# Two pairs of chunks at the start of a state-space and PReLU kernel: C in blocks turned by VectorE, and running products picked by a selection matmul

## The chip, the cores and the metric

The kernel runs on one core of a Trainium2 chip. The metric is the device time of one execution in microseconds (us); lower is better. Engines are named as in the profile: PE is TensorE (matmuls), PEld its weight loads, DVE is VectorE, ACT is ScalarE, POOL is GpSimd, and SP is SyncE, which issues most DMAs; ACT issues four small ones at the start.

## What is computed

Two blocks follow each other. The first is a chunked state-space scan over 4 batches, 8 heads, 768 tokens, head width 32 and 16 states; the second is a feed-forward layer with a PReLU of one slope per hidden unit:

```python
# first block, per batch and head, chunk by chunk
cum = cumsum(log(clip(a)))                 # within the chunk
L   = exp(cum_i - cum_j) * (i >= j)        # products of a between two tokens
y_i = sum_j (C_i . B_j) L_ij x_j  +  (C_i . state) * exp(cum_i)
state = exp(cum_last) * state + sum_j B_j x_j * exp(cum_last - cum_j)
# second block, on y as 3072 tokens x 256
h = y @ w_in                               # 256 x 2048
g = max(h, 0) + alpha * min(h, 0)
out = g @ w_out                            # 2048 x 256
```

All data is fp32.

## The kernel before, in words

The kernel cuts the tokens into chunks of 128 and works on them in twelve pairs. Two pairs make a group of 512 tokens for the feed-forward layer. Almost the whole span is the feed-forward layer on PE, with the pairs of later groups worked off between its matmuls. All engines run in the order in which the program is written (a manual schedule); an engine that waits holds everything behind it.

The first two pairs have a path of their own, `first_two` (line 821). They are cut into four quarters of 64 tokens each. For pair 0 it goes like this:

- `load_pair(0)` issues the loads. B and C come token by token, 64 bytes per head and token (line 192), x likewise in 128 bytes (line 197), a once as rows of 128 tokens (`rows`, 96 of them, line 126) and once repeated over the 16 states of each head (`ap`, line 133).
- `spread` (line 865) copies each head's a to all 64 tokens of a quarter by matmuls, and `scan` (line 871) on DVE makes the products of a between two tokens (`dec`).
- `rows_short` (line 488) scans the 96 rows twice on DVE: `pr` holds products from a token to its quarter's end, `rpf` the running products from the quarter's start. `pr` is turned by PE and copied by ACT (`prt`, line 511), and POOL multiplies B by it (`bn`, line 533).
- The running products are also needed with one row per head and state. For pair 0 they come from a scan of `ap` on DVE (`pf0`, line 1000). For pair 1 `rpf` is written to memory (`short`, line 500) and read back repeated over the states (`load_second`, line 231).
- `turned` (line 837) turns B and C on PE (line 843) into two PSUM banks, and ACT copies them to `bc` (line 847), C first; `spread_c` (line 854) makes two masked copies of C on ACT (`cz`).
- `gram_of` (line 881) multiplies B and C on PE, `times` (line 887) multiplies the result by `dec` on DVE, `added` (line 895) makes the new states' sums on PE, `states` (line 910) adds them up on DVE with the running products, `mask` (line 916) spreads them on POOL, `decayed_c` (line 961) multiplies C by the running products on POOL, and `x_products` (line 929) and `state_products` (line 941) make y on PE, which ACT copies to `xT` (lines 949 and 950).

Pair 1 follows in the same way, interleaved with the conversion of the first weights. A piece of w_in arrives as `raw`; ACT makes `wt` and `wg` (lines 273 and 283), DVE `wr` (lines 296 and 308), POOL or DVE clamps `wt` (line 278), and POOL adds the halves into `w_in` (line 330). `hidden_two` (line 1110) starts the feed-forward matmuls of the first 256 tokens; it stands before and around pair 1's work, and its second call runs pair 1's `gram_of` and y matmuls between its own. `keep_warm` (line 338) are matmuls on constants whose result nobody reads.

In PSUM, `spare()` gives one of two banks of the tag `hp`; a bank's first 256 columns and the rest are used for different things, for instance B's turned copy in front and `keep_warm` or the states' sums (`dps_in`) behind.

Of the kernel before, what the change touches and what calls it, by code (L numbers as in the profile page):

```python
# [22 lines left out]
def kernel(  # L23
# [32 lines left out]
    P = 128  # L56
# [82 lines left out]
    def load_tokens(dst, src, t0):  # L139


        d = dst.rearrange("p j (h w) -> p j h w", h=H)
        for k in range(2):
            for j in range(2):
                t = t0 + k * Q + j * HQ
                nc.sync.dma_start(out=d[HQ * k : HQ * (k + 1), j],
                                  in_=src[:, t : t + HQ, :].rearrange("h p w -> p h w"))
# [22 lines left out]
    def load_pair(gp, decays=True, parted=False):  # L170


        b, c = divmod(2 * gp, CPB)
        turned = gp > GC
        nat = ldx.tile([P, 3, 2, H * N], F32, name="nat")
        xt = ldx.tile([P, 2, HD], F32, name="xt")

        ap = ldx.tile([P, 2 * Q], F32, name="ap")
        if gp == 0:
            load_a(ap, b, c)  # L180
        elif gp > NB:
            load_products(gp, ap)
        if gp == 0:
            load_rows(0, nc.scalar)
        abc = []
        if gp >= HALF:
            load_tokens(nat[:, 0], B[b], c * Q)
        def load_bc(k):
            ts = slice((c + k) * Q, (c + k + 1) * Q)
            for i, src in enumerate((B,) if turned else (B, C)):  # L190
                eng = nc.scalar if gp == 0 and i else nc.sync
                eng.dma_start(out=nat[:, i, k].rearrange("p (h n) -> p h n", h=H),  # L192
                              in_=src[b, :, ts, :].rearrange("h p n -> p h n"))

        def load_x(k):
            ts = slice((c + k) * Q, (c + k + 1) * Q)
            nc.sync.dma_start(out=xt[:, k].rearrange("p (h d) -> p h d", h=H),  # L197
                              in_=x[b, :, ts, :].rearrange("h p d -> p h d"))

        for k in range((1 if parted else 2) if gp < HALF else 0):  # L200
            load_bc(k)
            if gp >= NB:
                load_x(k)
        for k in range(2 if gp < NB else 0):
            load_x(k)
        if gp == 0:
            nc.scalar.dma_start(out=al_n, in_=moe_alpha.rearrange("(k p) -> k p", p=P))
            loads["a", 1] = prep.tile([P, 2 * Q], F32, name="a1")
            load_a(loads["a", 1], b, c + 2)
        for i, src in enumerate((B, C) if turned else ()):  # L210


            for e in range(2):
                first = src[b, e : e + 1, c * Q : (c + 2) * Q, :]
                nc.sync.dma_start(out=nat[:, 1 + e, i],
                                  in_=bass.AP(tensor=first.tensor, offset=first.offset,
                                              ap=[[2 * S * N, P // 32], [8 * N, 32], [1, 8 * N]]))
        for k in range(2 if gp >= NB else 0):
            abc.append(lda.tile([P, H * Q], F32, name="abc"))
        loads["p", gp] = nat, abc, xt, ap  # L220
        if gp >= HALF:
            load_tokens(xt, x[b], c * Q)
        if decays:
            for part in load_spread(gp, b, c):
                pass
        return lambda: load_bc(1), lambda: load_x(1)

    def load_second():

        rows = scratch["short", 0].rearrange("(b h c) t -> b h (c t)", b=2, h=H)  # L230
        nc.sync.dma_start(out=loads["p", 1][3], in_=rows[0, :, 2 * Q : 4 * Q].unsqueeze(1)
                          .to_broadcast([H, N, 2 * Q]))

    al_n = const.tile([NF, P], F32, name="al_n")
    load_pair(0)
# [99 lines left out]
    def keep_warm(to, n, cols=2 * Q):  # L335

        for i in range(n):
            nc.tensor.matmul(to[:, :cols], warm.to_broadcast([P, P]), warm.to_broadcast([P, cols]),
                             start=True, stop=True, skip_group_check=True)
# [11 lines left out]
    lent = [gp.tile([P, 4, Q], F32, name="gt", tag="gt") for i in range(4)]  # L351
    starts_r = lent[3][:, 1]
    nc.gpsimd.memset(starts_r, 0.0)
    starts_a = lent[0][:, :2].rearrange("p k t -> p (k t)")
    nc.gpsimd.memset(starts_a, 0.0)
    bmask = const.tile([P, HD], F32, name="bmask")
    nc.gpsimd.memset(bmask, 1.0)
    bm3 = bmask.rearrange("p (h d) -> p h d", h=H)
# [7 lines left out]
    nc.vector.reduce_sum(out=par, in_=bm2[:, :, :, 0], axis=mybir.AxisListType.X)  # L366
    hmask = bmask[:, :P]
    nc.gpsimd.tensor_tensor(out=hmask, in0=hmask, in1=bmask[:, P:], op=ALU.add)
    zeros = const.tile([P, Q], F32, name="zeros")
    nc.gpsimd.memset(zeros, 0.0)  # L370
    ends = const.tile([P, Q], F32, name="ends")
# [14 lines left out]
    def slopes(alp):  # L386
        over = const.tile([P, NF], F32, name="over")
        nc.gpsimd.tensor_scalar(out=over, in0=alp, scalar1=1.0, scalar2=None, op0=ALU.is_gt)
        nc.gpsimd.tensor_scalar(out=s_mul, in0=over, scalar1=-2.0, scalar2=1.0, op0=ALU.mult,
                                op1=ALU.add)  # L390
        nc.gpsimd.tensor_tensor(out=s_alpha, in0=alp, in1=s_mul, op=ALU.mult)
# [44 lines left out]
    def clamp(eng, out, in_):  # L436
        eng.tensor_scalar(out=out, in0=in_, scalar1=1e-6, scalar2=1.0, op0=ALU.max, op1=ALU.min)
# [50 lines left out]
    def rows_short(r):  # L488


        nc.vector.memset(r[:, ::HQ], 0.0)
        pr = lent[3][:RW, 2]
        nc.vector.tensor_tensor_scan(out=pr[:, ::-1], data0=r[:, 1:][:, ::-1],
                                     data1=ends_q[:RW, ::-1], initial=0.0, op0=ALU.mult,
                                     op1=ALU.add)
        rpf = lent[3][:RW, 3]
        nc.vector.tensor_tensor_scan(out=rpf, data0=r[:, :Q], data1=starts_r[:RW], initial=0.0,
                                     op0=ALU.mult, op1=ALU.add)
        scratch["short", 0] = dr.tile([RW, Q], F32, name="short0")
        nc.sync.dma_start(out=scratch["short", 0], in_=rpf)  # L500
        return pr

    def rows_turn(i, pr):

# [316 lines left out]
    def first_two():  # L821
# [4 lines left out]
        nat0, _, xt0, ap0 = loads["p", 0]  # L826
        dec = [work.tile([P, 2, H, Q], F32, name="dec").rearrange("p k h t -> p (k h t)")
               [:, : 8 * Q].rearrange("p (r c) -> p r c", r=4) for i in range(2)]
        pf0 = lent[0][:, 2:].rearrange("p k t -> p (k t)")
        new = [lent[2][:, 2 * i : 2 * i + 2].rearrange("p k (c m) -> p (k c) m", c=2)  # L830
               for i in range(2)]
        sm = xsp.tile([P, 4, HT], F32, name="xs")
# [1 line left out]
              for i in range(2)]  # L834
        halves = [slice(HQ * j, HQ * (j + 1)) for j in range(2)]

        def turned(nat, banks, warmed=False):


            bc = work.tile([P, 4, Q], F32, name="bc")  # L840
            for k in range(2):
                for i, tp in enumerate(banks):
                    nc.tensor.transpose(tp[:, k * P : (k + 1) * P], nat[:, i, k], ident)
                if warmed and k == 0:
                    keep_warm(banks[0][:, 2 * Q :], 1)
            for i in (1, 0):
                nc.scalar.copy(out=bc[:, 2 * i : 2 * i + 2].rearrange("p k t -> p (k t)"),
                               in_=banks[i][:, : 2 * Q])
            return bc

        def spread_c(bc):
            cz = czp.tile([P, 2, 2, Q], F32, name="cz")
            for e in range(2):
                nc.scalar.mul(cz[:, e].rearrange("p k t -> p (k t)"),
                              bc[:, 2:].rearrange("p k t -> p (k t)"), par[:, e : e + 1])
            return cz
# [116 lines left out]
        clamp(nc.vector, rq[:, :Q], rows)  # L973
        z0 = first_a(ap0, nc.vector, lent[1][:, :2])
        clamp(nc.gpsimd, starts_r[:RW, ::HQ], rows[:, ::HQ])
        clamp(nc.gpsimd, starts_a[:, ::HQ], ap0[:, ::HQ])
        rows_clamp(0)
        sp = [bank(r) for r in range(4)]
        spread(z0, sp)
        prq = rows_short(rq)  # L980
        rows_out(0)
        load_pair(1)
        load_second()
        nat1, _, xt1, pf1 = loads["p", 1]
        for r in range(4):
            scan(0, r, sp[r])
        rows_turn("short", prq)
        tp, hp = spare(), spare()
        bc0 = turned(nat0, (tp, hp), True)
        cz0 = spread_c(bc0)  # L990
        al_p = ss()
        nc.tensor.transpose(al_p[:, :NF], al_n, ident[:NF, :NF])
        keep_warm(al_p[:, Q:], 1, 3 * Q)
        nc.scalar.copy(out=alpha, in_=al_p[:, :NF])
        bn0 = pair_loads(0)
        slopes(alpha)
        gram_of(bc0, cz0, sp)
        dps = dps_in([hp, tp])
        added(dps, bn0, xt0)
        nc.vector.tensor_tensor_scan(out=pf0, data0=z0.rearrange("p k t -> p (k t)"),  # L1000
                                     data1=starts_a, initial=0.0, op0=ALU.mult, op1=ALU.add)
        cd0 = decayed_c(bc0, pf0)
        for r in (0, 1):
            times(0, r, sp[r])
        states(0, dps, pf0)
# [27 lines left out]
        convert_b(*pieces[1])  # L1033
        for r in (2, 3):
            scan(1, r, sp[r])
        bn1 = pair_loads(1)
        convert_next(first=False)
        own = [ss(), ss()]
        second = spare()
        bc1 = turned(nat1, (sp[0], second))  # L1040
        cz1 = spread_c(bc1)
        dps = dps_in(own)
        mask(0, slice(3, 4))
        slope_signs()
# [535 lines left out]
```

## Time and profile before

| What | Value |
|---|---|
| three runs | 356.01, 356.4 and 356.7 us; median 356.4 |
| profiled execution, from the first to the last instruction | 355.9 us |
| granted TensorE clock | 1.000 |
| PE busy | 349.3 us (98%) |
| DVE, POOL, ACT busy | 235.8, 204.4 and 171.8 us |
| DMA packets | 105581, of them 79896 under 512 bytes |

The page gives the profiled execution by its span. The runs' median lies 0.5 us above that span, and what lies around the span is taken as that 0.5 us. The chain of waits names for each moment the work that the end depended on; "SPq" in it is the issuing of DMAs. The busy time of PE contains matmuls that run behind one another in a pipeline, so that a busy share near 100% does not by itself say that no time is lost.

### The profile page before, as it was taken

How to read it: one execution, taken by the hardware profiler on the slowest of the kernel's cores; microseconds unless marked ns; L12 is line 12 of the kernel's file. 1: busy time of each engine (PE TensorE's matmuls, PEld its weight loads, DVE VectorE, ACT ScalarE, POOL GpSimd, SP SyncE). 2: the span in 40 equal slices, each digit the busy share in tenths (PEclk: the TensorE clock that was granted, in tenths of full speed). 3: DMA queues.
4: the chain of work that ended last, by engine and by line, in shares of the span. 5: the costliest groups of instructions: out<-in, count | busy, mean ns of one | idle time of the engine just before them, and what ended most of it. 6: DMA issues, size and time to landing. Idle time of an engine off the chain costs nothing.

```text
span 355.9 us, 7778 instructions
## 1 busy us (share of the span) xinstructions
PE 349.3 (98%) x2985; PEld 284.4 (80%) x2985; DVE 235.8 (66%) x482; ACT 171.8 (48%) x391; POOL 204.4 (57%) x228
## 2 busy tenths in 40 slices
PE   8899999999999999999999999999999999999996
PEld 4576665578788888888888888888888888888885
DVE  6876986998748756847747856757856633643363
ACT  3477576535355346345345445345445344443431
POOL 6776568589939855725646626637526535434520
PEclk9999999999999999999999999999999999999999
DMA  7899989607345403503423423422001001001102
GB/s 138 182 202 270 329 174 279 148 17 159 106 83 128 102 3 75 104 2 77 78 57 74 86 51 71 85 55 65 11 2 31 0 2 29 2 1 31 31 0 59
DMA packets 105581, 30.24 MB, mean 85 GB/s; under 512 B 79896, under 2 KB 101448, under 8 KB 105544
## 3 DMA queue, kind: packets, MB, share of 16 engines
q1 hardware_dynamic: 103048, 29.43, 36.3%
q10 hardware_dynamic: 2496, 0.32, 0.6%
q8 instruction: 23, 0.38, 0.5%
q14 instruction: 14, 0.11, 0.1%
HBM read 26.32 MB, written 3.42 MB: 84 GB/s over the span
## 4 chain that ended last, share of the span: by engine, by line
PE 89%; SPq 4%; DMA 3%; DVE 2%; ACT 1%; POOL 1%; issue 0%; DVEq 0%; ACTq 0%
PE bank L1216 33%; PE hp L1241 29%; PE bank L1142 6%; PE ss L1241 6%; PE hp L1095 3%; DMA raw<-in_moe_w_in_dram 2%; SPq L192 2%; PE ss L787 1%; PE ss L731 1%; PE hp L1110 1%; PE bank L1209 1%; PE ss L805 1%; PE ss L779 1%; DMA xt<-in_x_dram 1%; SPq L197 1%; PE ss L742 1%
## 5 line engine op out<-in xcount | busy, mean ns | idle before, releaser
L1298 POOL TENSOR_TENSOR gt<-gt 128x512 f32<-128x512 f32 x58 | 74.2, 1279 | 21.1 <-DVE gt L1226 16.3
L1216 PE MATMUL bank<-gt,w_out 128*128 128x256 f32 x320 | 83.5, 381 | 0.0
L1216 PEld LDWEIGHTS bank<-gt,w_out 128*128 128x128 f32 x320 | 60.1, 190 | 9.2 <-issue 1.0
L1288 POOL TENSOR_TENSOR gt<-gt 128x512 f32<-128x512 f32 x20 | 25.4, 1269 | 62.5 <-DVE gt L1226 49.7
L1226 DVE SCALAR_TENSOR_TENSOR gt<-hp,s_mul,gt 128x256 f32<-128x256 f32 x96 | 42.0, 479 | 29.1 <-ACT gt L1224 26.8
L1224 ACT ACTIVATE gt<-hp,s_alpha 128x256 f32<-128x256 f32 x96 | 40.3, 471 | 34.5 <-PE hp L1241 31.4
L1216 PE MATMUL bank<-gt,ws 128*128 128x256 f32 x224 | 55.9, 379 | 0.0
L1216 PEld LDWEIGHTS bank<-gt,ws 128*128 128x128 f32 x224 | 42.3, 190 | 5.6
L1241 PE MATMUL hp<-xs,w_in 128*128 128x256 f32 x160 | 41.9, 384 | 0.0
L1241 PE MATMUL hp<-xs,ws 128*128 128x256 f32 x160 | 41.1, 380 | 0.0
L1267 DVE TENSOR_TENSOR hp<-hp,u 128x512 f32<-128x512 f32 x20 | 14.0, 700 | 35.2 <-ACT u L1265 35.2
L1241 PEld LDWEIGHTS hp<-xs,ws 128*128 128x128 f32 x160 | 30.3, 190 | 4.3 <-POOL xs L1183 0.2
L1241 PEld LDWEIGHTS hp<-xs,w_in 128*128 128x128 f32 x160 | 29.7, 190 | 4.5
L1142 PE MATMUL bank<-w_out,gt 128*128 128x256 f32 x128 | 31.1, 385 | 0.4 <-POOL w_out L330 0.4
L1142 PEld LDWEIGHTS bank<-w_out,gt 128*128 128x128 f32 x128 | 23.6, 190 | 7.2 <-issue 2.9
L1241 PE MATMUL ss<-xT,w_in 128*128 128x256 f32 x96 | 24.6, 379 | 0.0
L645 POOL TENSOR_TENSOR sm<-state,bmask 128x256 f32<-128x256 f32 (+1 forms) x10 | 6.2, 620 | 29.0 <-DVE state L642 29.0
L1095 PE MATMUL hp<-xT,w_in 128*128 128x512 f32 x48 | 22.8, 596 | 0.0
L561 DVE TENSOR_TENSOR_SCAN dec<-abc,bank 128x192 f32<-128x192 f32 x48 | 22.7, 522 | 0.0
L1256 ACT COPY m<-hp 128x512 f32<-128x512 f32 x8 | 4.7, 586 | 35.7 <-PE hp L1241 35.7
L1265 ACT COPY u<-hp 128x512 f32<-128x512 f32 x20 | 11.7, 585 | 19.4 <-PE hp L1241 19.4
L1226 DVE SCALAR_TENSOR_TENSOR gt<-c,s_mul,gt 128x256 f32<-128x256 f32 x40 | 20.6, 555 | 0.0
(232 smaller groups left out, 608.2 us busy)
## 6 DMA issues: line engine op xcount, KB each, us to landing
abc<-z SPq DMA_DIRECT2D x24, 192.0 KB
raw<-in_moe_w_in_dram SPq DMA_DIRECT2D x8, 512.0 KB
raw<-in_moe_w_out_dram SPq DMA_DIRECT2D x8, 512.0 KB
abc<-z SPq DMA_DIRECT2D x8, 512.0 KB
out_dram<-o_sb SPq DMA_DIRECT2D x32, 64.0 KB
nat<-in_B_dram SPq DMA_DIRECT2D x26, 64.0 KB
xt<-in_x_dram SPq DMA_DIRECT2D x12, 128.0 KB
xt<-in_x_dram SPq DMA_DIRECT2D x24, 64.0 KB
```

What stands on the lines that cost most here:

```text
L192: eng.dma_start(out=nat[:, i, k].rearrange("p (h n) -> p h n", h=H), in_=src[b, :, ts, :].rearrange("h p n -> p h n"))
L561: nc.vector.tensor_tensor_scan(out=dv[:, o : o + SQ], data0=abc[k][:, s : s + SQ], data1=ident_p[0][:, :SQ], initial=0.0, op0=ALU.mult, op ...
L1095: nc.tensor.matmul(hp, w_in[:, k, f * P : (f + 1) * P], xts[g][:, k], start=(k == 0), stop=(k == KC - 1))
L1142: nc.tensor.matmul(pos[0][t // 2][:, t % 2], gt[:, t * Q : (t + 1) * Q], w_out[:, f], start=(f == 0 and t % 2 == 0), stop=(f == NF - 1), s ...
L1216: nc.tensor.matmul(ms[g][i][:, h], w, blocks[g, z][n][:, p], start=(q == 0 and h == 0), stop=(q == NQ - 1), skip_group_check=True)
L1224: nc.scalar.mul(o[:, p], h[:, p], s_alpha[:, fs[p]])
L1226: nc.vector.scalar_tensor_tensor(out=o[:, p], in0=h[:, p], scalar=s_mul[:, fs[p]], in1=o[:, p], op0=ALU.mult, op1=ALU.max)
L1241: nc.tensor.matmul(to[:, p], w(2 * z + p), b, start=start and p == 0, stop=True, skip_group_check=True)
L1265: nc.scalar.copy(out=u2, in_=A)
L1267: nc.vector.tensor_tensor(out=Y, in0=Y, in1=u2, op=ALU.add)
L1288: nc.gpsimd.tensor_tensor(out=tc_, in0=g22, in1=g12, op=ALU.subtract)
L1298: eng.tensor_tensor(out=o, in0=x0, in1=x1, op=ALU.subtract)
```

## The change

For pairs 0 and 1, C is now loaded in blocks of eight tokens (512 bytes; two DMAs per pair in place of two), the form in which the later pairs are loaded, and turned by one DVE transpose per pair, `turn_c`; B is still turned by PE (`turn_b`). The running products of both pairs no longer come from a scan of `ap` (pair 0) or through memory (pair 1): a matrix `pick` of zeros and ones, made on POOL, selects and repeats the rows of `rpf` in four 128-column matmuls, two for each pair (`products_of`), and ACT copies the two results. One `keep_warm` of 384 columns goes, POOL's clamp into `starts_a` goes, and `added` stands before `gram_of` in pair 0.

```diff
-            for i, src in enumerate((B,) if turned else (B, C)):
-                eng = nc.scalar if gp == 0 and i else nc.sync
+        if gp < NB:
+            load_blocks(lambda e: nat[:, 1, e], C, nc.scalar if gp == 0 else nc.sync)
+            for i, src in enumerate((B,) if turned or gp < NB else (B, C)):
...
-    def load_second():
-        rows = scratch["short", 0].rearrange("(b h c) t -> b h (c t)", b=2, h=H)
-        nc.sync.dma_start(out=loads["p", 1][3], in_=rows[0, :, 2 * Q : 4 * Q].unsqueeze(1)
-                          .to_broadcast([H, N, 2 * Q]))
...
-    starts_a = lent[0][:, :2].rearrange("p k t -> p (k t)")
-    nc.gpsimd.memset(starts_a, 0.0)
+    pick = lent[0][:RW]
+    nc.gpsimd.memset(pick, 0.0)
...
     nc.gpsimd.tensor_tensor(out=hmask, in0=hmask, in1=bmask[:, P:], op=ALU.add)
+    pick4 = pick.rearrange("p k (h n) -> p k h n", h=H)
+    nc.gpsimd.affine_select(out=pick4, in_=pick4, pattern=[[-1, 4], [-CPB, H], [0, N]],
+                            compare_op=ALU.not_equal, fill=1.0, base=0, channel_multiplier=1)
...
-        scratch["short", 0] = dr.tile([RW, Q], F32, name="short0")
-        nc.sync.dma_start(out=scratch["short", 0], in_=rpf)
-        return pr
+        return pr, rpf
...
+        def turn_c(nat):
+            bc = work.tile([P, 4, Q], F32, name="bc")
+            nc.vector.transpose(
+                bc[:, 2:].rearrange("p k t -> p (k t)").rearrange("p (c b) -> p b c", b=8),
+                nat[:, 1].rearrange("p e (b n) -> p b e n", n=N))
+            return bc
+        def turn_b(bc, nat, tp):
+            for k in range(2):
+                nc.tensor.transpose(tp[:, k * P : (k + 1) * P], nat[:, 0, k], ident)
+            nc.scalar.copy(out=bc[:, :2].rearrange("p k t -> p (k t)"), in_=tp[:, : 2 * Q])
+        def products_of(c, tp):
+            pf = prep.tile([P, 2 * Q], F32, name=f"pf{c}")
+            for k in range(2):
+                nc.tensor.matmul(tp[:, k * P : (k + 1) * P], pick[:, c + k], rpq,
+                                 start=k == 0, stop=True, skip_group_check=True)
+            nc.scalar.copy(out=pf, in_=tp[:, : 2 * Q])
+            return pf
...
-        clamp(nc.gpsimd, starts_a[:, ::HQ], ap0[:, ::HQ])
...
         load_pair(1)
-        load_second()
+        bc0 = turn_c(nat0)
+        cz0 = spread_c(bc0)
         for r in range(4):
             scan(0, r, sp[r])
         rows_turn("short", prq)
         tp, hp = spare(), spare()
-        bc0 = turned(nat0, (tp, hp), True)
-        cz0 = spread_c(bc0)
+        turn_b(bc0, nat0, tp)
+        keep_warm(tp[:, 2 * Q :], 1)
+        pf0 = products_of(0, hp)
+        pf1 = products_of(2, ss())
         al_p = ss()
         nc.tensor.transpose(al_p[:, :NF], al_n, ident[:NF, :NF])
-        keep_warm(al_p[:, Q:], 1, 3 * Q)
         nc.scalar.copy(out=alpha, in_=al_p[:, :NF])
         bn0 = pair_loads(0)
+        cd0 = decayed_c(bc0, pf0)
         slopes(alpha)
-        gram_of(bc0, cz0, sp)
         dps = dps_in([hp, tp])
         added(dps, bn0, xt0)
-        nc.vector.tensor_tensor_scan(out=pf0, data0=z0.rearrange("p k t -> p (k t)"),
-                                     data1=starts_a, initial=0.0, op0=ALU.mult, op1=ALU.add)
-        cd0 = decayed_c(bc0, pf0)
+        gram_of(bc0, cz0, sp)
...
         for r in (2, 3):
             scan(1, r, sp[r])
+        bc1 = turn_c(nat1)
+        cz1 = spread_c(bc1)
         bn1 = pair_loads(1)
         convert_next(first=False)
         own = [ss(), ss()]
         second = spare()
-        bc1 = turned(nat1, (sp[0], second))
-        cz1 = spread_c(bc1)
+        turn_b(bc1, nat1, second)
```

More of the change, by code (lines that the diff above doesn't have):

```diff
@@ L187, in load_pair, with load_blocks @@
             load_tokens(nat[:, 0], B[b], c * Q)
+        def load_blocks(to, src, eng=nc.sync):
+            for e in range(2):
+                first = src[b, e : e + 1, c * Q : (c + 2) * Q, :]
+                eng.dma_start(out=to(e),
+                              in_=bass.AP(tensor=first.tensor, offset=first.offset,
+                                          ap=[[2 * S * N, P // 32], [8 * N, 32], [1, 8 * N]]))
+        if gp < NB:
+            load_blocks(lambda e: nat[:, 1, e], C, nc.scalar if gp == 0 else nc.sync)
         def load_bc(k):
             ts = slice((c + k) * Q, (c + k + 1) * Q)
-            for i, src in enumerate((B,) if turned else (B, C)):
-                eng = nc.scalar if gp == 0 and i else nc.sync
-                eng.dma_start(out=nat[:, i, k].rearrange("p (h n) -> p h n", h=H),
-                              in_=src[b, :, ts, :].rearrange("h p n -> p h n"))
+            for i, src in enumerate((B,) if turned or gp < NB else (B, C)):
+                nc.sync.dma_start(out=nat[:, i, k].rearrange("p (h n) -> p h n", h=H),
+                                  in_=src[b, :, ts, :].rearrange("h p n -> p h n"))
         def load_x(k):
@@ L210, in load_pair @@
         for i, src in enumerate((B, C) if turned else ()):
[L213 to L217, printed above, removed]
+            load_blocks(lambda e: nat[:, 1 + e, i], src)
         for k in range(2 if gp >= NB else 0):
@@ L828, in first_two @@
                [:, : 8 * Q].rearrange("p (r c) -> p r c", r=4) for i in range(2)]
-        pf0 = lent[0][:, 2:].rearrange("p k t -> p (k t)")
         new = [lent[2][:, 2 * i : 2 * i + 2].rearrange("p k (c m) -> p (k c) m", c=2)
@@ L835, in first_two @@
         halves = [slice(HQ * j, HQ * (j + 1)) for j in range(2)]
-        def turned(nat, banks, warmed=False):
+        def turn_c(nat):
             bc = work.tile([P, 4, Q], F32, name="bc")
-            for k in range(2):
[L842 to L849, printed above, removed]
+            nc.vector.transpose(
[3 more added lines that the diff above has]
+        def turn_b(bc, nat, tp):
+            for k in range(2):
+                nc.tensor.transpose(tp[:, k * P : (k + 1) * P], nat[:, 0, k], ident)
[7 more added lines that the diff above has]
+            return pf
         def spread_c(bc):
@@ L979, in first_two @@
         spread(z0, sp)
-        prq = rows_short(rq)
+        prq, rpq = rows_short(rq)
         rows_out(0)
         load_pair(1)
-        load_second()
-        nat1, _, xt1, pf1 = loads["p", 1]
+        nat1, _, xt1, _ = loads["p", 1]
+        bc0 = turn_c(nat0)
+        cz0 = spread_c(bc0)
         for r in range(4):
```

## The prediction

> **What bounds the kernel now.** First the busy time of the engines on the page (busy us, share, instructions), which names PE.
>
> ```profile
> PE 349.3 (98%) x2985; PEld 284.4 (80%) x2985; DVE 235.8 (66%) x482; ACT 171.8 (48%) x391; POOL 204.4 (57%) x228
> ```
>
> Then two stretches; the columns are length, busy time of PE, PEld, DVE, ACT and POOL, granted clock, DMA share and GB/s.
>
> ```profile
> 23.20:46.00 22.80, 22.35 (x102) 14.46 (x101) 17.70 (x35) 16.11 (x35) 14.72 (x16) 1.00 0.96 276
> 46.00:355.90 309.90, 306.50 (x2500) 257.32 (x2500) 200.01 (x399) 145.94 (x333) 173.42 (x173) 1.00 0.30 65
> ```
>
> From 46 us on PE is busy for 306.50 of 309.90 us, and from 23.2 to 46 for 22.35 of 22.80. The change touches nothing there, so the end moves by what PE is late or early on leaving the first two pairs, at 23.28 us, less what later stalls give back. The chain in order of time (start, length, what) shows how PE gets there, and that later stall.
>
> ```profile
> 14.22 3.28 DMA xt<-in_x_dram
> 17.54 0.35 PE ss L895 x16
> 17.89 0.63 PE hp L338 x2
> 18.52 0.86 PE hp L1110 x4
> 19.38 0.65 PE bank L881 x32
> 29.84 7.45 DMA raw<-in_moe_w_in_dram
> 44.52 1.28 POOL w_out L330
> 45.84 1.99 PE bank L1142 x8
> ```
>
> Pair 1's x lands at 17.50 and starts `added`, the second keep_warm, L1110 and gram in turn. At 45.8 a chain that began with a weight's load ends; PE loses about 0.45 us there (45.4 to 45.84), and a later PE loses that much less. Last, the timeline by engine (start, busy time, engine, line, operation, and in brackets the idle time before it with its releaser).
>
> ```profile
> 4.02 0.24 POOL L437 TENSOR_SCALAR gt<-rows 96x2 f32<-96x2 f32 x1
> 4.55 0.39 DVE L497 TENSOR_TENSOR_SCAN gt<-rq,gt 96x128 f32<-96x128 f32 x1
> 5.55 2.43 DVE L871 TENSOR_TENSOR_SCAN dec<-bank,ident_q 128x256 f32<-128x256 f32 x4 [0.61 <-PE bank L865]
> 5.79 0.24 ACT L511 COPY prt<-ss 128x96 f32<-128x96 f32 x1 [0.81 <-PE ss L506]
> 7.30 0.92 ACT L854 ACTIVATE cz<-bc,par 128x256 f32<-128x256 f32 x2
> 8.97 0.76 DVE L887 TENSOR_TENSOR dec<-bank,dec 128x256 f32<-128x256 f32 x2 [0.40 <-PE bank L881]
> 12.24 0.43 DVE L278 TENSOR_SCALAR wt<-wt 128x512 f32<-128x512 f32 x1 [0.28 <-ACT wt L273]
> 13.28 1.69 POOL L330 TENSOR_TENSOR w_in<-wr,wg 128x256 uint32<-128x256 uint32 x2 [2.13 <-ACT xT L949]
> 16.31 1.26 DVE L871 TENSOR_TENSOR_SCAN dec<-bank,ident_q 128x256 f32<-128x256 f32 x2
> 17.06 0.37 ACT L847 COPY bc<-hp 128x256 f32<-128x256 f32 x1 [2.51 <-PE hp L843]
> 18.30 0.98 DVE L910 SCALAR_TENSOR_TENSOR gt<-gt,ap,ss 128x64 f32<-128x64 f32 x3 [0.72 <-DMA ap<-short]
> ```
>
> The reader should see that in pair 1 DVE is busy with scans until 17.57, while ACT copies C at 17.06, straight after PE turned it. C's new way lies behind those scans.
>
> **The price of the new steps.** The turn on DVE handles 128x256 elements, read and written with strides. Its nearest rows are L574, the same operation and pattern at 128x512, with 1108 to 1120 ns, and L1392, contiguous, with 702 for 128x512 and 434 for 128x256. I take half of L574's with a little for the start, 0.60 us; bounds 0.43 and 1.11. A pick costs two fp32 matmuls of 128 columns: a 256-column fp32 pass took 0.21 us here (eight L1110 in 1.73), so 0.43 for the two and their filling, then ACT's copy of 0.37 (L847), or 0.25 to 0.3 where it follows other work on ACT (17.06 to 17.33). POOL's select over 96x512 has as rows 0.29 us for 128 columns (the identity's, at 1.07) and 0.45 for 256 (L361): 0.16 per 128 columns, 0.77 at 512. The memset for `pick` covers 512 columns where `starts_a` had 256; memset rows of 0.20 (128) and 0.31 (256) give 0.22 more.
>
> **Pair 0.** POOL comes first. Before its `starts_r` clamp (L437, ending 4.27) now stand the memset's 0.22 and the select's 0.77: it ends at about 5.2. The second scan of the rows waits for it and ends at 5.65 in place of 4.94. The new turn stands behind that on DVE, 6.25, provided that both C loads have landed (C was there for PE at 5.59). ACT runs in order, so `cz` (0.92) from 6.25 to 7.2 now holds the copy of `prt` (7.4, before 6.03) and B's copy (0.25, 7.65). Behind B's copy waits keep_warm, which writes the other half of B's bank; it cannot start before that copy in the changed program. Queued behind it on PE are both picks, alpha's turn, `added` and gram.
>
> keep_warm's 0.60 gives 8.3, the picks 8.8, `pf0`'s copy 9.2. `added`, which shares the pick's bank, runs from 9.45 to 10.0 and gram from 9.95; before, gram ran from 8.27. `times` follows 0.7 after gram's start: 10.6 in place of 8.97, +1.65. The next link takes some back: the first weight's clamp on DVE (L278) waited 0.28 us for ACT's `wt` at 12.24 and comes at 13.6, +1.35. The weights' adds on POOL (L330) go from 13.28 to 14.65, and the scans of pair 1, behind the same DVE work, end at 18.95 in place of 17.57. PE's first L1110 moves along.
>
> **Pair 1.** `turn_c` is put behind the fourth scan: 18.95 + 0.60 = 19.5, with a little between. `cz` 0.92, 20.45; only then ACT copies B, to 20.7, although PE has long turned it. The second keep_warm goes into B's bank and waits; queued behind it on PE are L1110's last 256-column passes, gram and y of pair 1 and all else. It started at 17.82 (17.89 on the chain) and would at 20.75: +2.9. PE busy behind it is unchanged. At 45.84 0.45 comes back: **+2.45**, 355.9 + 2.45 = 358.35 of span. The runs' median lies 0.5 above the span: **358.8 us**.
>
> What I put at nothing: 0.67 us of `pf0`'s DVE scan and 0.91 of keep_warm go, but DVE and PE then wait for the chain through POOL, ACT and B's copy; without that cover the scan would give 0.67. C's loads become 512-byte packets; 3584 packets of 64 bytes go with `short` and its read. x of pair 1 lands earlier and the 0.72 us wait for `ap` ends; next late there is the copy of B. `decayed_c` of pair 0 stands before `slopes` on POOL, and its wait for `pf0` (9.2) holds the slopes and masks to about 12.1, which pair 0's y, late by 1.65 itself, covers; without that cover it would cost about 1. The two C loads are issued by ACT and SP at the old places and in the old number.
>
> **Bounds.** Low: turns of 0.43, a select of 0.45 as L361, C early: pair 0 +0.9, pair 1 +1.3 on top, 2.2 less 0.45, +1.75, and 358.1. High: turns of 1.11, and C at 6.5 us rather than 5.6: about 1.5 to 2 more than the forecast, 360.4 at most. Should POOL's select cost nothing and the L278 link absorb all of pair 0, pair 1's own wait remains: 17.57 + 0.43 + 0.92 + 0.25 = 19.2, 1.3 past 17.89; less 0.45 and a little more given back at 45.8 that is +0.8, and 357.2.
>
> [...] The row on the shared bank: in the profile of before no matmul waits for a copy there, since ACT's copy of `hp` ended at 17.43 and keep_warm into `hp` started at 17.82. [...] On the clock: PE's longest idle time near pair 1 is 0.85 us before L1110 (14.11), with 1.00 granted. By my sum PE would idle up to 1.9 us. [...]
>
> **Rivals.** *The loads decide* (faster). If the second keep_warm starts when x is there, the earlier x and the weights count. PE's L1110 passes still wait for POOL's add, 18.11, against 18.52 on the chain: 0.35 at most, and 0.44 at 45.8, 0.79 in all: 355.1 of span, **355.6**. For it: the chain passes through x's DMA. Against it: it decides only if B's copy is done by 17.8, so with 0.43 + 0.92 + 0.25 = 1.6 the turn must start at 16.2, while the scans before it ended at 17.57 even before. *The clock drops* (slower still). In the first microseconds four 512-column passes of L338 took 3.75 us (0.83 to 4.58), while L1095 has 0.60 for one later; a gap of 1.9 could bring that back, for 3.75 - 2.4 = 1.4 us more: **360.2**. Against it: 0.85 did nothing. *Nothing moves* (no change): the loss is given back at 45.8 and by earlier loads. For it the loss has to stay under 0.45 + 0.2; **356.4**.
>
> **How the numbers follow.** A median within 0.2% (0.7 us) of before can hardly be told from no change. The forecast gets 0.78, the faster rival 0.11, the clock 0.07, no change 0.04. Slower is 0.78 + 0.07 = 0.85. The range goes from 357.2 to 360.4, the bounds above; it takes in the clock's case and leaves out the faster rival and no change (0.15), and with them a forecast missed by more than its bounds.
>
> **What would show it.** In the profile after: POOL's `starts_r` clamp ends near 5.2; two DVE transposes of about 0.6 us; the first keep_warm after B's copy at 7.7; gram of pair 0 near 9.95 and `times` at 10.6; L330's first add near 14.6; scans of pair 1 until 19; the second keep_warm at 20.7, with ACT's copy as releaser and no wait for x or `ap`; PE leaves pair 1 near 26.2. It is wrong if gram of pair 0 starts before 8.8, if the second keep_warm starts before 19, or if the PE stall at 45.8 grows.

## The result, and the profile after

The changed kernel takes **364.65 us** (median of six runs, 364.24 to 364.87) against 356.55 for the kernel before (six runs): 2.3% slower, ratio 1.0228 with a 95% interval of 1.0209 to 1.0247. The direction was forecast; the size, +2.4 us, was not: +8.1 were measured, and the range ended at 360.4.

The profiled execution has a span of 362.5 us and a time of 364.24, 1.74 more. The same difference, 1.6 to 1.8, stands beside nearly every run of every kernel here, the kernel before among them (span 354.8 at 356.49, below). So the 0.5 us of the prediction was wrong: by this measure the span of 355.9 belongs to an execution of some 357.6 us, slower than the median. Spans below are set against 354.8.

The busy time by stretches after the change (columns as in the prediction):

```profile
8.50:14.80 6.30, 5.70 (x107) 4.51 (x107) 2.21 (x7) 2.16 (x7) 2.65 (x7) 1.00 0.75 193
24.00:28.00 4.00, 3.94 (x39) 2.76 (x40) 0.17 (x1) 1.86 (x5) 2.43 (x5) 0.57 0.92 222
30.70:46.00 15.30, 15.30 (x69) 10.83 (x68) 12.98 (x25) 13.13 (x30) 10.80 (x13) 1.00 0.87 273
46.00:362.50 316.50, 313.05 (x2533) 260.98 (x2531) 206.44 (x409) 149.30 (x338) 177.05 (x177) 1.00 0.29 64
```

From 30.7 us on PE loses as little as before; the loss lies ahead of that. And the granted clock, the share of its full speed that PE was given, is 0.57 from 24 to 28. The chain in order of time shows where the end now comes from:

```profile
2.43 4.00 DMA nat<-in_C_dram
...
6.53 0.65 DVE bc L838
...
7.21 0.91 ACT cz L861 x2
...
8.24 0.28 ACT bc L847
...
8.57 1.22 PE hp L336 x2
...
22.21 0.54 DVE bc L838
...
22.85 0.71 ACT cz L861 x2
...
23.66 0.36 ACT bc L847
...
24.06 1.22 PE hp L336 x2
25.28 1.71 PE hp L1117 x4
```

The steps are the forecast ones: C's turn, its spread, B's copy, keep_warm (L336), twice over. But the same two 256-column passes of keep_warm take 1.22 us here and 0.60 to 0.70 before. The timeline after, with the waits ahead of those two places and lines of POOL and DVE; below it one line of the kernel before:

```profile
4.10 1.09 POOL L368 TENSOR_SCALAR_AFFINE_SELECT gt<-gt 96x512 f32<-96x512 f32 x1
...
6.69 0.48 PE L846 MATMUL hp<-ident,nat 128*128 128x128 f32 x1 [0.34 <-DMA nat<-in_B_dram]
8.57 1.22 PE L336 MATMUL hp<-const-float32-1.0 128*128 128x256 f32 x2 [1.40 <-ACT bc L847]
...
12.25 1.20 PE L888 MATMUL bank<-cz,bc 32*64 32x128 f32 x32
13.41 0.76 DVE L894 TENSOR_TENSOR dec<-bank,dec 128x256 f32<-128x256 f32 x2 [4.02 <-PE bank L888]
...
22.13 0.62 DVE L838 STREAM_TRANSPOSE bc<-nat 128x256 f32<-128x256 f32 x1
...
24.06 1.22 PE L336 MATMUL hp<-const-float32-1.0 128*128 128x256 f32 x2 [2.02 <-ACT bc L847]
```

```profile
8.27 0.73 PE L881 MATMUL bank<-cz,bc 32*64 32x128 f32 x32 [0.53 <-ACT alpha L994]
```

PE idles 1.40 us and 2.02 us, each time for ACT's copy of B. Behind both, PE runs at half speed: gram of pair 0 takes 1.20 where it took 0.73.

How PE came to half speed differs between the two places. It starts at half speed in both kernels (four 512-column passes in 3.75 us from 0.83 us; four later ones, L1095 of the kernel before, in 1.91). In the kernel before it is at full speed when it turns B and C (270 to 329 ns each, from 5.59 us). In this execution the two turns of B, at 5.93 and 6.69 us and so ahead of the first wait, take 421 and 476 ns: PE had not come up to full speed when it had to wait, and stays at half speed until about 17.3 (the two 512-column passes from 14.80 us take 2.07, where they took 1.13 from 10.14). At the second place it does fall: the granted clock is 1.00 up to 24.0 us, 0.50 from there to 27.4, and 1.00 again. For the first stretch the profile reads 1.00 (8.50 to 14.80 above) although the passes are slow, as it does for the first passes of both kernels; a low clock ahead of the first change on record is not in that reading. In five other runs of this kernel, with 0.981 for the whole span, about 2 x 0.019 x 363 = 13.8 us at half clock are on record. That is more than the 3.4 us of the second place, so in those runs part of pair 0's slow stretch probably came as a fall, of which `e11` below shows one. The time is the same either way, 364.24 and 364.35 to 364.87.

### The profile page after: what moved, and what is told of

It reads as the page before. It is cut to its first block, busy times and chain, and to the rows that moved or that the text cites. A ratio compares the mean times of both kernels' runs of the same rounds, so it can differ in the third digit from the quotient of the medians.

```text
span 362.5 us, 7779 instructions
## 1 busy us (share of the span) xinstructions
PE 353.7 (98%) x2987; PEld 287.9 (79%) x2987; DVE 237.1 (65%) x483; ACT 172.3 (48%) x391; POOL 205.5 (57%) x228
## 4 chain that ended last, share of the span: by engine, by line
PE 94%; DVE 2%; DMA 1%; ACT 1%; issue 1%; POOL 1%; ACTq 0%; POOLq 0%; DVEq 0%
PE bank L1223 33%; PE hp L1248 28%; PE bank L1149 8%; PE hp L1102 6%; PE ss L1248 6%; PE ss L786 1%; PE hp L1117 1%; PE ss L730 1%; DMA nat<-in_C_dram 1%; PE bank L1216 1%; PE ss L804 1%; PE ss L778 1%; PE ss L741 1%; PE hp L336 1%; PE ss L617 1%
```

## The experiments

Theory 1 is that the waits are as forecast and that on top of them PE's clock is low behind them because PE idles. Theory 2 is that the waits, or the new steps themselves, make up the whole loss. Fillers are extra keep_warms that nobody reads. Where runs of one kernel differ, their granted clocks stand beside them. Ratios are to the kernel before, with 95% intervals.

**Fillers in both places** (`e1`), **in pair 0** (`e2`), **in pair 1** (`e3`).

```diff
 # e1, e2: inside turn_b of pair 0, between the two turns of B
+                if fill is not None and k == 0:
+                    keep_warm(fill, 1)
 # e1, e2: pair 0 (fill = hp[:, 2 * Q :])
+        keep_warm(hp[:, 2 * Q :], 3)
         keep_warm(tp[:, 2 * Q :], 1)
 # e1, e3: pair 1
+        keep_warm(sp[0][:, 2 * Q :], 4)
         keep_warm(second, 1)
```

> The changed kernel with fillers only: one keep_warm between the two turns of B of pair 0 and three after them, in the picks' bank, and four ahead of the second keep_warm, in a bank of pair 1's spread; no wait of the change is taken away. Theory 1 (the clock): PE's passes ran at half speed from 8.57 to 17.2 us and again from 24.06 to 27.4 because PE idled (1.40 and 2.02 us) before; with fillers pair 0's times start near 10.6 in place of 13.41 and the second keep_warm near 20.8, and the median is 3.2 + 1.5 lower, 359.9 us (359 to 361). Theory 2 (the waits alone set the time; slow passes lie beside other waits): within 0.7 of the changed kernel, 364.0 to 365.3.

> The changed kernel with the fillers of pair 0 alone. Theory 1: pair 0 at full clock, the gap of 2 us in pair 1 stays and the clock drops there: 3.2 lower, about 361.4 us. Theory 2: unchanged, 364.65 within 0.7.

> The changed kernel with the four fillers ahead of the second keep_warm alone. Theory 1: pair 0 as slow as in the changed kernel, second keep_warm still near 24.1, but its passes at 0.21 in place of 0.43: 1.5 lower, about 363.1 us. Theory 2: unchanged, 364.65 within 0.7.

Measured: 359.86, 360.13 and 362.75 us, ratios to before 1.0100 [1.0077, 1.0123], 1.0108 [1.0080, 1.0136] and 1.0185 [1.0148, 1.0223]. Adding work to PE takes 4.8, 4.5 and 1.9 us off. The waits stay: PE's timeline of the kernel with the fillers of pair 0 has the idle 2.02 us again, and full speed on both sides. In pair 0 of that profile the first turn of B is still slow (0.42 us at 5.94), and behind the first filler PE is at full speed (six 256-column passes in 1.47 us from 6.88).

```profile
8.64 0.70 PE L336 MATMUL hp<-const-float32-1.0 128*128 128x256 f32 x2 [0.29 <-ACT bc L849]
...
10.71 0.76 PE L890 MATMUL bank<-cz,bc 32*64 32x128 f32 x32
...
21.12 0.70 PE L336 MATMUL hp<-const-float32-1.0 128*128 128x256 f32 x2 [2.02 <-ACT bc L849]
```

So theory 1 holds, but `e2` lies 1.3 us under its forecast, and the terms don't add up: 4.5 and 1.9 apart, 4.8 together. With pair 0 at full clock the 2.02 us of pair 1 do no harm in two runs of four: these runs of `e2` have clocks of 1.000 and 0.999 and 359.7 and 359.6 us; the two others 0.995 and 360.5 and 361.3. The same 2.02 us are followed by a clock of 0.50 in the changed kernel's profile and of 1.00 in that of `e2` (from 20 to 28 us). The four runs of `e3` have 361.9 to 364.8 us at clocks of 0.991 to 0.981, but one has 362.7 at 1.000; a low clock ahead of the first change on record would not show in that reading.

**One filler, the one between B's turns** (`e11`, the changed kernel with the first hunk above alone).

> The changed kernel with one keep_warm between the two turns of B of pair 0, where the kernel before has one; the idle time ahead of the keep_warm in B's bank (1.40 us) and the one in pair 1 (2.02) stay. Theory 1 (it is the long idle time that brings the clock down, not the short one of 0.34 us between the turns): PE may be at full clock by 6.9 us, falls again behind the idle time, and at most 1.5 us come back: 363.2 to 364.9. Theory 2 (once warm, the clock stays; the missing filler is the loss): as with all fillers of pair 0, about 360.1.

Measured: 364.53 us, ratio 1.0207 [1.0138, 1.0276], as theory 1 has it. Here the first rise comes early, and the profile shows the low clock of pair 0 (two stretches, then PE's two waits for B's copy):

```profile
8.50:14.80 6.30, 5.74 (x108) 4.60 (x109) 2.50 (x8) 2.16 (x6) 2.95 (x8) 0.53 0.78 197
18.00:22.00 4.00, 4.00 (x44) 3.10 (x45) 2.28 (x5) 1.98 (x6) 1.57 (x3) 0.50 0.99 201
```

```profile
8.53 0.93 PE L336 MATMUL hp<-const-float32-1.0 128*128 128x256 f32 x2 [1.95 <-ACT bc L849]
...
26.04 0.70 PE L336 MATMUL hp<-const-float32-1.0 128*128 128x256 f32 x2 [1.97 <-ACT bc L849]
```

PE had been at full speed (keep_warm 0.60 at 5.87), idled 1.95 us up to 8.53, fell at 8.9 and stayed at half clock until 22.5. Full speed ahead of the wait did not protect it here. Yet 1.97 us of idling in pair 1 of the same execution left it at full speed: the length of the wait alone did not decide. Its four runs follow the clock: 360.94 us at 0.994, 364.48 and 364.59 at 0.981, 366.23 at 0.976.

**The kernel before without two fillers** (`e4`): the keep_warm between the turns and the one of 384 columns are taken out of pair 0.

> The kernel before without two keep_warms of pair 0 (the one between the turns of B and C, 0.60 us, and the one of 384 columns, 0.91); nothing reads them. Theory 1: PE idles in place of them, its clock is low in pair 0, and the kernel loses 2 to 3.5 us: 358.5 to 360 us. Theory 2: the fillers cost or bring nothing, 356.5 within 0.7.

Measured: 356.75 us, ratio 1.0015 [0.9992, 1.0037]; theory 1 was wrong by its number. PE idled 1.38 us, the clock fell (0.993 to 0.995 in eight of ten runs), and two 512-column passes of keep_warm took 2.02 in place of 1.13; yet the first feed-forward matmuls started at 14.10, as before (14.11).

```profile
8.22 0.82 PE L879 MATMUL bank<-cz,bc 32*64 32x128 f32 x32 [1.38 <-ACT alpha L991]
```

They need the first weight. In the kernel before the engines wait for it to land, at 11.5 us (ACT idles 1.82 us for it, and PE 0.85 us ahead of these matmuls); in this profile it had landed by 10.5, and DVE, busy with pair 0, came to it at 11.69. So the low clock used up time that the kernel before spends waiting for the weight. The two runs with the lowest clocks, 0.990 and 0.984, have 357.7 and 359.1 us: there a longer low stretch seems to cost. In the changed kernel pair 0 is late enough for a low clock to cost from its start.

**The two halves apart, and the kernel before again.** `e6` has C's half with the fillers of pair 0 (old scan of `ap`, old `short`, no `pick`); `e7` the picks in the kernel before, C as it was.

```diff
 # e7, in the kernel before
+        pf0 = products_of(0, ss())
+        pf1 = products_of(2, ss())
         bn0 = pair_loads(0)
```

> The kernel before once more, for the span of a profiled execution beside these runs. Theory 1: a span of some 1.7 us under its time, as the changed kernel and the experiments so far have it (354.6 to 354.9), so that the 0.5 us of the prediction was a matter of its one profile. Theory 2: a span of 355.9 again, and 1.2 us of the loss lie outside the span.

> C's half of the change alone, with the fillers of pair 0: C in blocks turned by DVE, the products of a from the old scan and through memory, no select on POOL and no picks. Theory 1: pair 0 sheds the picks (0.86) and the select, the turn behind pair 1's scans stays: about 0.8 under the fillers alone, 359.3 us. Theory 2 (the picks are the cost): back near the kernel before, 356.3 to 357.3.

> The other half alone, in the kernel before: products of a picked by matmuls, C as it was. Theory 1: B, C and their copies keep their times, PE has no gap and the clock holds; 0 to 1 us over the kernel before, 356.3 to 357.3. Theory 2 (the picks are the cost): 2 us and more over it, from 358.3.

Measured: the kernel before 356.41 us with a span of 354.8, no stall of PE at 45.8, and pair 1 left at 23.07; C's half 359.43, ratio 1.0089 [1.0056, 1.0122]; the picks 356.6, ratio 1.0012 [0.9994, 1.0030], no difference that shows. The loss hangs on C's half: its load in blocks, its turn, and the copies that stand behind it. Next to `e2` C's half is 0.7 us faster at clock 1.000 (358.95 and 358.98 against 359.60 and 359.74), so with the turn in place the picks and the select do cost something. C's half without fillers was not run.

**C of pair 1 turned earlier** (`e5`, with the fillers of pair 0):

```diff
         scan(1, 1, sp[1])
+        bc1 = turn_c(nat1)
+        cz1 = spread_c(bc1)
         convert_b(*pieces[1])
         for r in (2, 3):
             scan(1, r, sp[r])
-        bc1 = turn_c(nat1)
-        cz1 = spread_c(bc1)
```

> The changed kernel with the fillers of pair 0 (the clock stays full) and the turn of C of pair 1 ahead of the third scan, where DVE waited for POOL. Theory 1 (with the clock held, what is left in pair 1 is the turn behind the scans, then C's spread, then B's copy on ACT): B's copy near 19.0, the second keep_warm near 19.1 and L1117 behind POOL's add at 19.8 in place of 21.66; 1.9 lower than with the fillers alone, about 358.2 us. Theory 2 (something else in pair 1 is as late): 360.1 within 0.7.

Measured: 358.27 us (seven runs, 358.20 to 358.37), ratio 1.0046 [1.0029, 1.0063], 1.9 under `e2`'s median and 1.4 under its two runs at full clock; the rest is the low clock of its other two. The timeline has the turn 1.7 us earlier (17.46 against 19.19) and keep_warm too; DVE's work on the weight and the last two scans start 0.5 to 0.6 us later for it:

```profile
17.46 0.61 DVE L838 STREAM_TRANSPOSE bc<-nat 128x256 f32<-128x256 f32 x1
...
18.98 0.35 ACT L849 COPY bc<-hp 128x256 f32<-128x256 f32 x1
...
19.38 0.70 PE L336 MATMUL hp<-const-float32-1.0 128*128 128x256 f32 x2 [0.33 <-ACT bc L849]
20.14 1.13 PE L1120 MATMUL hp<-xT,w_in 128*128 128x256 f32 x4
```

**No hold on B's bank** (`e9`): with the fillers of pair 0, two instead of three, the keep_warm in B's bank is taken out.

> The changed kernel with fillers in pair 0 as before, but without the keep_warm in B's bank, so that the picks wait for no copy (two fillers in place of three). Theory 1 (pair 0 is late by the hold on B's copy): the picks run near 7.9 in place of 9.2, added starts near 9.1 in place of 10.3, and of this 1.0 to 1.3 us come through: 358.9 us (358.6 to 359.3), against 360.1 with the fillers alone. Theory 2 (pair 0 is late by C's landing and its spread; the hold only lies beside them): 360.1 within 0.7.

Measured: 359.65 us (358.49 to 361.12), ratio 1.0092 [1.0065, 1.0118], not clear by its median. By clock it is: the one run at 1.000 has 358.49, 1.2 under `e2` at the same clock and just below theory 1's range; the three at 0.995 and 0.990 have 359.4 to 361.1. `added` ran at 8.97 (10.32 in `e2`), so the hold is shown. In the profiled run, one of the three, the clock fell behind pair 1's wait, from 20.1 to 23.5 us (0.57 from 20 to 24); in the other two only the lower clock of the whole span is known.

**All waits taken away** (`e8`), **the turn of pair 0 put later too** (`e12`), **and `e8` without fillers** (`e13`). `e8` joins `e5` and `e9`, and:

```diff
+        # select for `pick` after the clamps of rows_clamp(0)
         turn_b(bc0, nat0, tp, hp[:, 2 * Q :])
+        cz0 = spread_c(bc0)
-        added(dps, bn0, xt0)
         gram_of(bc0, cz0, sp)
+        added(dps, bn0, xt0)
 # e12 in addition
+        for r in (0, 1):
+            scan(0, r, sp[r])
         bc0 = turn_c(nat0)
-        for r in range(4):
+        for r in (2, 3):
             scan(0, r, sp[r])
```

> The whole change with its new waits taken away: no keep_warm in B's bank, the select after the rows' clamps on POOL, B's copy ahead of C's spread on ACT and gram ahead of added in pair 0, C of pair 1 turned ahead of the third scan, fillers in pair 0. Theory 1 (the loss is these waits and the clock, nothing else): within 1 us of the kernel before, 355.8 to 357.3. Theory 2 (the new steps themselves cost): still over 358.

> The repaired kernel with the turn of C of pair 0 after the second scan in place of ahead of the first. Theory 1 (what the repaired kernel still loses, 0.7 us, is the wait for C's blocks, 1.18 us, ahead of DVE's four scans): the scans start near 5.9 in place of 7.02, and 0.4 to 0.8 come back: 356.2 to 356.6, the same as the kernel before. Theory 2 (pair 0 is late by its picks on PE and ACT): 357.0 within 0.2.

> The repaired kernel without its two fillers. Theory 1 (idle time under a limit between 1.0 and 1.4 us in one stretch does not bring the clock down; PE would idle some 0.3 us between B's turns and up to 0.5 behind them): full clock from 7 us on, 357.0 within 0.4. Theory 2 (without fillers the clock stays or falls low in pair 0): 358 to 361.

Measured: `e8` 357.04 us, ratio 1.0017 [1.0006, 1.0027]; `e12` **356.31** (eleven runs 356.2 to 356.9, one 358.5 at clock 0.995), ratio 1.0004 [0.9990, 1.0018]; `e13` 358.20 (356.97 to 359.99), ratio 1.0046 [1.0023, 1.0069]. In `e12` DVE's scans no longer wait for C's blocks (they started at 7.02 in `e8`):

```profile
5.79 1.27 DVE L877 TENSOR_TENSOR_SCAN dec<-bank,ident_q 128x256 f32<-128x256 f32 x2 [0.46 <-PE bank L871]
6.98 0.61 DVE L835 STREAM_TRANSPOSE bc<-nat 128x256 f32<-128x256 f32 x1
```

With that the whole change costs nothing that shows, and brings nothing. `e13` went against theory 1: its runs at clock 1.000 have 357.0, one at 0.998 has 358.1, those at 0.990 have 358.3 and 358.4, those at 0.985 have 359.9 and 360.0. In its profile (0.985) the clock falls at 9.4 us (0.68 from 8 to 12, 0.50 from 12 to 16), and the longest idle time of PE ahead of that is this one:

```profile
6.76 0.33 PE L843 MATMUL hp<-ident,nat 128*128 128x128 f32 x1 [0.50 <-DMA nat<-in_B_dram]
```

So here the clock fell without a single long wait: from 4 to 12 us PE idled 0.85 us in all (busy for 3.30 and 3.85 of 4.00 each). With its two fillers `e8` has 356.9 to 357.2 in all eleven runs, without them three of eight do; `e12` without fillers was not run.

**C of pair 1 alone, in the kernel before** (`e10`), loaded in blocks and turned ahead of the third scan.

> The kernel before with C of pair 1 alone loaded in blocks and turned by DVE ahead of the third scan; all else as before. Theory 1: PE sheds two turns of 0.11, C's spread and B's copy are in time, x lands earlier: 0 to 0.5 under the kernel before, 355.8 to 356.3. Theory 2 (a turn on DVE delays pair 1 wherever it stands): 0.6 over it and more, from 356.9.

Measured: 356.57 us, ratio 1.0003 [0.9995, 1.0012]: no change. The two PE turns that it saves (0.11 us each) don't show. No version here beats the kernel before.

## Why the prediction was right and wrong

**Right: what waits for what.** Every link was there: POOL's select ahead of `starts_r`, the turn ahead of pair 0's scans and behind pair 1's, B's copy behind C's spread, keep_warm behind B's copy. The turn took 0.62 to 0.64 us (0.60 forecast). With the clock held (`e1`) PE left pair 1 at 26.26 us on the chain; the forecast was 26.2. Some of that is luck: the second keep_warm came at 21.12 (20.75 forecast), and from there to the end of pair 1 PE took 5.1 us, where 5.4 had been taken over from the profile before.

**Wrong: the clock.** The step that failed is the one on PE's idle times: for up to 1.9 us of them, the author's estimate, the prediction adds nothing. No run shows that term; in its place the runs show half clock in pair 0 up to 17.3 us and again from 24.0 to 27.4, worth 4.8 us (`e1` against the changed kernel). The only row of the kernel before on this is 0.85 us of idling at full clock, less than half as long; and the step took for granted that PE comes to full speed ahead of pair 0's wait, as it did before. The rival on the clock was there, with a chance of 0.07, but its 1.4 us price one stretch behind pair 1's wait alone, not pair 0.

The runs differ: 1.38 us of idling (`e4`), 1.95 (`e11`) and 2.02 in the changed kernel were followed by a fall, 1.97 in pair 1 of `e11` and 2.02 in `e2` were not. So do the low stretches: 3.4 us in the changed kernel (24.0 to 27.4) and in `e4` (0.59 from 8 to 12 us, 0.98 from 12 to 16), but 13.65 in `e11`, where the clock falls at 8.87 and rises at 22.52. Why the same idle time brings the clock down in one execution and not in another stays open.

**Wrong: pair 0's own delay, in two sizes.** The select took 1.09 us, not 0.77, and C's blocks landed at 6.43, not near 5.6. The 5.59 of the prediction is the turn of C's first half; the second half landed at 5.97 in that profile. And ACT took longer to issue the first load (1.15 us in place of 0.45), so that the second one started at 2.43 in place of 1.71; from there it took 4.00 us, against 4.26. So `starts_r` was done at 5.66 (5.2 forecast), the turn at 7.17 (6.25), B's copy at 8.51 (7.65). PE thus idled 1.40 us, where the forecast's times gave about 0.9 (from 6.73, the end of B's turn before, to 7.65). This lengthened the very wait behind which the clock was low.

**Wrong: the 0.45 us to come back at 45.8.** That stall belonged to the one execution profiled; the second profile of the kernel before has none. With the clock held the loss is therefore 358.0 - 354.8 = 3.2 us of span, against 2.9 forecast ahead of that term.

**The sum.** From the changed kernel to the kernel before, medians: 4.5 come back with the clock of pair 0 held (`e2`), 1.9 with pair 1's turn ahead of the scans (`e5`), 1.2 with the hold, the select, ACT's order and gram's place in pair 0 (`e8`), 0.7 with pair 0's turn behind two scans (`e12`): 8.3, where 8.1 were lost. The steps are differences of one row of medians, so their sum only says again that `e12` is as fast as the kernel before; each share holds for this order, and of the 1.9 some 0.5 is the low clock of two of `e2`'s runs.

**The other rivals.** Earlier loads: x was there (17.07 for its second half) well ahead of PE, and it gained nothing, since B's copy stood ahead. The hold on B's bank did bind in pair 0 (`e9`: `added` at 8.97 without it, 10.32 in `e2`); in pair 1 keep_warm and L1117 write the very columns that B's copy reads, and keep_warm waited 2.02 us for that copy. And the 1.73 us that the prediction gives for eight L1110 belong to eight L1142; eight L1110 took 1.74, and the price of 0.21 a pass stands.

## What to carry to other kernels

A wait that was put ahead of TensorE had two prices here: its own length (1.40 and 2.02 us), and the half clock at which the matmuls behind it ran (4.8 us, `e1` against the changed kernel). Look for the second in single passes of a known shape (here 0.43 against 0.21 us per 256 columns), since the granted clock read 1.00 from 8.50 to 14.80 us although such passes were slow, and test with fillers before anything else. The transposition moved to VectorE was worth no more than its place there: ahead of the third scan, in a gap of DVE, it was free (`e10`), behind four scans it cost 1.4 us at full clock (`e2` against `e5`).

## What the runs showed of the hardware

- The clock fell with 1.4 to 2.0 us of idling in one piece (`e4`, `e11`, the changed kernel's pair 1), and in the profile of `e13` with pieces of at most 0.5 us. But it did not fall with 0.85 us (the kernel before), nor with 1.97 and 2.02 us in pair 1 of `e11` and `e2`.
- PE started at half speed (3.75 us for four 512-column passes, later 1.91). In the kernel before it was at full speed by 5.6 us; in the changed kernel's profile, with its waits, not before about 17.3.
- Once low it stayed low through work with gaps: 13.65 us in `e11`, although PE was busy for 12.94 of the 13.50 us from 8.5 to 22.0.
- A low clock of some 3.4 us (0.59 from 8 to 12 us, 0.98 from 12 to 16) cost nothing clear where the engines waited for a weight anyway (`e4`, ratio 1.0015). `e2`'s two runs at 0.995 (an estimated 2 x 0.005 x 358 = 3.6 us at half clock) took 0.8 to 1.7 us more than its two at full clock.
- C in blocks of 512 bytes landed later than in tokens of 64 bytes (6.43 against 5.97 us for pair 0's second half), because its load was issued later (from 2.43 us in place of 1.71); from the start of the load it took 4.00 against 4.26 us. Each of these block loads of C left 5 landing marks (signs of the DMA that a part has landed), each token load 16.
